# Weights first in SBUF and the other tiles 64 bytes behind multiples of 2048: a change of addresses alone in a convolution and squared-ReLU MLP kernel

## The chip, the cores and the metric

One core of one Trainium2 chip. The metric is the device time of one execution in microseconds (us); lower is better. The engines are named as in the profile: PE is TensorE's stream of matmuls, PEld its loads of stationary operands (weights), DVE is VectorE, ACT ScalarE, POOL GpSimd, SP SyncE. SBUF is the on-chip memory from which the engines read: 128 partitions side by side, and in each partition a row of bytes. An address below is the byte at which a tile begins in each partition.

## The reference, cut to what matters

```python
def _attn_ref(x, weight):            # x (8, 4096, 192), weight (8, 7)
    w = exp(weight - max(weight, -1)); w = w / (sum(w, -1) + 1e-09)
    x_pad = concatenate([zeros((B, 6, D)), x], axis=1)
    # out[b, s, h*24+g] = sum over k of w[h, k] * x_pad[b, s + k, h*24+g]

def _moe_ref(x, w_in, w_out, s, b):  # 32768 tokens, 192 -> 2048 -> 192
    h = x @ w_in
    r = np.maximum(h, 0.0)
    g = s * (r * r) + b
    return (g @ w_out).astype(np.float32)
```

A causal convolution with seven taps over the sequence is followed by two matrix products with a squared ReLU between them. The inputs are float32.

## The kernel before, in words

**Precision.** The kernel computes with float32 words marked fp32r and splits each operand into a high part and a low part, so that one product is three matmuls (high by low, low by high, high by high). The token tiles `sA`, `wA`, `tB`, `wB` hold both parts of the convolved tokens (`wA` and `wB` with the two partition halves swapped, filled by DMA at L171 and L172). `qh` and `ql` hold the high and low parts of the squares.

**Tiling.** Tokens go in blocks of 512 columns (`BLK`), two blocks to a super-block `n`. The 2048 hidden features go in eight pairs `p` of 2 x 128. One step is a triple `(n, j, p)`. A step has two groups of matmuls. `first` (L531) makes `h` of 256 features: nine products for each of two halves of 64 rows, so 18 matmuls. `second` (L614) multiplies the squares of an earlier step (two steps behind, `LAG = 2`) by the output weights: ten products for each half, so 20 matmuls. Almost all matmuls thus have 64 rows and come in couples: one of the couple uses partitions 0 to 63, the other 64 to 127, both stream 512 columns (2048 bytes of each partition), and they run side by side. Each has a weight load of its own, 128 columns (512 bytes of each partition). A step is 19 couples; a block of eight steps is 152 couples. The first super-block is different: it is done while weights are still being prepared, and its `second_whole` (L576 to L583) uses matmuls of the full 128 rows.

**Around the matmuls.** ACT takes `h` from PSUM with a ReLU (L545) and squares it (L552), DVE makes `qh` (L554) and `ql` (L559) and convolves the next block (L161, L163), POOL adds up the output halves (L638 to L647), SP issues the DMAs. The order on PE, DVE and ACT is the order in which the program was written; `queue` holds the squares that wait for `second`. In the first super-block the convolution of one part is done on PE with plain float32 operands (L257, `conv_tensor`).

**Where the tiles lie.** Tile pools are laid out in SBUF in the order in which they are opened, one behind the other, each tile rounded up to 32 bytes. The constants end 864 bytes behind a multiple of 2048, and the unused tile `gap` (L81, 296 words, 1184 bytes) fills the rest up to address 18432, which is 9 x 2048. From there on the pools follow: `qs` (ten tiles of 4096 bytes for `qh` and `ql`), `xs` (tokens), `act` (`q`), `outs`, `wide_w` (the weights `W`, 40960 bytes, at 139264, and `WB`, 8192 bytes, at 180224), `raw`, `wordp`, `xin`. All tiles up to `WB` have sizes that are multiples of 2048, so all begin at multiples of 2048. A 128-column slice of `W` or `WB`, as one weight load reads it, begins at a multiple of 512: `W` has rows of 640 words (2560 bytes) per pair and part, in slices of 128 words, and `WB` has rows of 128 words (512 bytes). So the slices fall on all four offsets 0, 512, 1024 and 1536 from a multiple of 2048, while every stream of 512 columns begins at an offset of 0.

Of the kernel before, what the change touches and what calls it, by code (L numbers as in the profile page):

```python
# [9 lines left out]
F32 = mybir.dt.float32  # L10
# [7 lines left out]
P = 128  # L18
# [9 lines left out]
WARM = (BLK, BLK // 2, BLK // 2)  # L28

GAP = 296  # L30


TOP_MIN = struct.unpack("<f", struct.pack("<I", (1023 - 127) << 20))[0]
# [4 lines left out]
def conv_attention_then_squared_relu_mlp(  # L38
# [40 lines left out]
    bb = const.tile([P, 1], F32, name="bb")  # L79
    bias = const.tile([P, 3], F32, name="bias")  # L80
    const.tile([P, GAP], F32, name="gap")  # L81
    qs = ctx.enter_context(tc.tile_pool(name="qs", bufs=LAG + 3))
    xs = ctx.enter_context(tc.tile_pool(name="xs", bufs=2))
    act = ctx.enter_context(tc.tile_pool(name="act", bufs=3))
    outs = ctx.enter_context(tc.tile_pool(name="outs", bufs=3))
    wide_w = ctx.enter_context(tc.tile_pool(name="wide_w", bufs=1))
    raw = ctx.enter_context(tc.tile_pool(name="raw", bufs=2))
    wordp = ctx.enter_context(tc.tile_pool(name="wordp", bufs=3))
    xin = ctx.enter_context(tc.tile_pool(name="xin", bufs=2))
# [759 lines left out]
```

## Time and profile before

| | |
|---|---|
| median of 3 runs | 2234.84 us (2234.82 to 2234.86) |
| the profiled execution's own time | 2234.66 us |
| its span, first to last instruction | 2232.9 us |
| PE busy | 2226.4 us, 19330 matmuls |
| PEld busy | 1829.1 us, 19330 loads |
| DVE busy | 1753.5 us |
| ACT busy | 1286.4 us |
| POOL busy | 317.8 us |
| granted TensorE clock | 1.000 of full |

A row of a group gives the line, engine, operation, output and inputs, their shapes and count, then the group's busy time in us and the mean duration of one in ns, then the idle time of the engine before them. Two matmuls that run side by side are both counted with their full duration there. The end of a matmul is modelled in these profiles, so its duration says little; the distance from one start to the next says how fast PE goes. A row of the timeline or of the chain gives the start in us, the length in us and what ran, with the count where several alike are merged. The span begins at 0.

### The profile page before, as it was taken

How to read it: one execution, taken by the hardware profiler on the slowest of the kernel's cores; microseconds unless marked ns; L12 is line 12 of the kernel's file. 1: busy time of each engine (PE TensorE's matmuls, PEld its weight loads, DVE VectorE, ACT ScalarE, POOL GpSimd, SP SyncE). 2: the span in 40 equal slices, each digit the busy share in tenths (PEclk: the TensorE clock that was granted, in tenths of full speed). 3: DMA queues.
4: the chain of work that ended last, by engine and by line, in shares of the span. 5: the costliest groups of instructions: out<-in, count | busy, mean ns of one | idle time of the engine just before them, and what ended most of it. 6: DMA issues, size and time to landing. Idle time of an engine off the chain costs nothing.

```text
span 2232.9 us, 45081 instructions
## 1 busy us (share of the span) xinstructions
PE 2226.4 (100%) x19330; PEld 1829.1 (82%) x19330; DVE 1753.5 (79%) x1995; ACT 1286.4 (58%) x1410; POOL 317.8 (14%) x205
## 2 busy tenths in 40 slices
PE   9999999999999999999999999999999999999999
PEld 6788888888888888888888888888888888888887
DVE  8898778777787787777877878778777787787764
ACT  8755555655555555555555555555655555556554
POOL 0022101111011011110110111111101111011110
PEclk9999999999999999999999999999999999999999
DMA  5113112121121111211111111112121121111110
GB/s 180 34 43 87 40 46 62 48 58 44 44 58 53 53 44 45 56 53 53 43 51 50 53 53 53 48 43 62 51 55 44 44 58 53 53 44 42 46 39 17
DMA packets 46168, 117.51 MB, mean 53 GB/s; under 512 B 7760, under 2 KB 8016, under 8 KB 45968
## 3 DMA queue, kind: packets, MB, share of 16 engines
q1 hardware_dynamic: 45824, 114.50, 18.6%
q8 instruction: 151, 2.47, 0.5%
q14 instruction: 49, 0.40, 0.1%
q10 hardware_dynamic: 144, 0.13, 0.0%
HBM read 31.64 MB, written 25.17 MB: 25 GB/s over the span
## 4 chain that ended last, share of the span: by engine, by line
PE 98%; DVE 1%; ACT 1%; DMA 0%; issue 0%; SPq 0%; DVEq 0%
PE acc L614 50%; PE h L531 46%; DVE accA L163 0%; PE acc L576 0%; ACT q L552 0%; DVE ql L559 0%; PE acc L577 0%; PE acc L583 0%; PE acc L582 0%; PE acc L581 0%; ACT qh L554 0%; ACT q L545 0%; DMA xA<-in_xA 0%; DVE t L315 0%; ACT oC L589 0%
## 5 line engine op out<-in xcount | busy, mean ns | idle before, releaser
L545 ACT ACTIVATE q<-h 128x1024 f32<-128x1024 f32 x512 | 525.5, 1026 | 902.8 <-PE h L531 900.4
L559 DVE TENSOR_TENSOR ql<-q,qh 128x1024 fp32r<-128x1024 f32 x512 | 656.7, 1283 | 56.3 <-ACT qh L554 2.6
L554 DVE CAST qh<-q 128x1024 fp32r<-128x1024 f32 x497 | 370.1, 745 | 395.7 <-ACT q L552 393.3
L614 PE MATMUL acc<-qh,W 64*128 64x512 f32 x3960 | 609.9, 386 | 0.0
L552 ACT ACTIVATE q<-q 128x1024 f32<-128x1024 f32 x512 | 543.6, 1062 | 15.9
L614 PEld LDWEIGHTS acc<-qh,W 64*128 64x128 f32 x3960 | 370.9, 184 | 77.9
L531 PE MATMUL h<-sA,W 64*128 64x512 f32 x3072 | 432.4, 387 | 0.0
L531 PE MATMUL h<-wA,W 64*128 64x512 f32 x3072 | 431.6, 386 | 0.0
L531 PE MATMUL h<-tB,W 64*128 64x512 f32 x1536 | 429.9, 386 | 0.0
L531 PE MATMUL h<-wB,W 64*128 64x512 f32 x1536 | 429.9, 386 | 0.0
L614 PE MATMUL acc<-ql,WB 64*128 64x512 f32 x1980 | 385.7, 386 | 0.4 <-DVE ql L559 0.4
L614 PE MATMUL acc<-qh,WB 64*128 64x512 f32 x1980 | 385.6, 386 | 0.0
L614 PE MATMUL acc<-ql,W 64*128 64x512 f32 x1980 | 385.5, 386 | 0.0
L638 POOL TENSOR_TENSOR oB<-oB,oB 128x512 f32<-128x512 f32 x61 | 115.2, 1889 | 1672.7 <-ACT oB L637 1672.7
L163 DVE SCALAR_TENSOR_TENSOR accA<-xA,tap,accA 128x512 f32<-128x512 f32 x378 | 341.5, 903 | 6.8
L531 PEld LDWEIGHTS h<-sA,W 64*128 64x128 f32 x3072 | 287.3, 184 | 62.9 <-issue 1.1
L531 PEld LDWEIGHTS h<-wA,W 64*128 64x128 f32 x3072 | 287.8, 184 | 60.4
L531 PEld LDWEIGHTS h<-tB,W 64*128 64x128 f32 x1536 | 282.6, 184 | 40.5 <-issue 0.2
L531 PEld LDWEIGHTS h<-wB,W 64*128 64x128 f32 x1536 | 282.5, 184 | 20.1
L614 PEld LDWEIGHTS acc<-ql,WB 64*128 64x128 f32 x1980 | 185.5, 184 | 40.1 <-DVE ql L559 1.3
L614 PEld LDWEIGHTS acc<-ql,W 64*128 64x128 f32 x1980 | 185.5, 184 | 39.0
L614 PEld LDWEIGHTS acc<-qh,WB 64*128 64x128 f32 x1980 | 185.5, 184 | 38.8
(115 smaller groups left out, 1035.4 us busy)
## 6 DMA issues: line engine op xcount, KB each, us to landing
wA<-sA SPq DMA_DIRECT2D x126, 256.0 KB, 3.6
outT<-oA SPq DMA_DIRECT2D x63, 256.0 KB, 2.0
wB<-tB SPq DMA_DIRECT2D x60, 256.0 KB, 3.4
xA<-in_xA SPq DMA_DIRECT2D x24, 515.0 KB, 3.6
xB<-in_xB SPq DMA_DIRECT2D x32, 259.0 KB, 2.6
oC<-oB SPq DMA_DIRECT2D x61, 128.0 KB, 2.2
outT<-oC SPq DMA_DIRECT2D x60, 128.0 KB, 2.3
words<-in_w SPq DMA_DIRECT2D x7, 768.0 KB, 6.2
```

What stands on the lines that cost most here:

```text
L163: nc.vector.scalar_tensor_tensor(acc, src, w[:, k : k + 1], acc, op0=ALU.mult, op1=ALU.add)
L531: nc.tensor.matmul(h[:, i, :], w_in(w, p, chunk[0], rows), chunk[part], start=start, stop=stop)
L545: nc.scalar.activation(q, h, AF.Relu)
L552: nc.scalar.activation(q, q, AF.Square)
L554: cast(qh, q)
L559: nc.vector.tensor_tensor(ql, q, qh.bitcast(F32), op=ALU.subtract)
L614: nc.tensor.matmul(accs[to + 2 * i], w(f, r), q[r, f % 2, :], start=start and f == 0, stop=stop and f == ends[i],)
L638: nc.gpsimd.tensor_tensor(o[1], o[1], o[3], op=ALU.add)
```

## The change

The pool of the weights is opened right behind `gap`, so `W` and `WB` come first. Behind them comes a new unused tile of 16 words (64 bytes), and then the other pools in their old order.

```diff
 GAP = 296
+SHIFT = 16
...
     const.tile([P, GAP], F32, name="gap")
+    wide_w = ctx.enter_context(tc.tile_pool(name="wide_w", bufs=1))
+
+    shift = ctx.enter_context(tc.tile_pool(name="shift", bufs=1))
+    shift.tile([P, SHIFT], F32, name="shift")
     qs = ctx.enter_context(tc.tile_pool(name="qs", bufs=LAG + 3))
     xs = ctx.enter_context(tc.tile_pool(name="xs", bufs=2))
     act = ctx.enter_context(tc.tile_pool(name="act", bufs=3))
     outs = ctx.enter_context(tc.tile_pool(name="outs", bufs=3))
-    wide_w = ctx.enter_context(tc.tile_pool(name="wide_w", bufs=1))
     raw = ctx.enter_context(tc.tile_pool(name="raw", bufs=2))
```

Worked out from the sizes: `W` begins at 18432 (9 x 2048) and `WB` at 59392 (29 x 2048), so weight slices still begin at multiples of 512. `qs` begins at 67648, 64 bytes behind 33 x 2048, and `qh`, `ql`, the token tiles, `q` and the outputs all begin 64 bytes behind a multiple of 2048. `raw`, `wordp` and `xin` move up by 64 bytes. No instruction is added, removed or put in another place.

## The prediction

> **What bounds the kernel now.** I read the page's busy times and clock row first, then the chain that ended last, then one steady window, then the chain in order of time inside it.
>
> ```profile
> span 2232.9 us, 45081 instructions
> PE 2226.4 (100%) x19330; PEld 1829.1 (82%) x19330; DVE 1753.5 (79%) x1995; ACT 1286.4 (58%) x1410; POOL 317.8 (14%) x205
> ...
> PEclk9999999999999999999999999999999999999999
> ...
> PE 98%; DVE 1%; ACT 1%; DMA 0%; issue 0%; SPq 0%; DVEq 0%
> PE acc L614 50%; PE h L531 46%; DVE accA L163 0%; PE acc L576 0%; ACT q L552 0%; DVE ql L559 0%; PE acc L577 0%; PE acc L583 0%; PE acc L582 0%; PE acc L581 0%; ACT qh L554 0%; ACT q L545 0%; DMA xA<-in_xA 0%; DVE t L315 0%; ACT oC L589 0%
> ```
>
> PE is busy all the time at the full granted clock, and 96% of the chain are the matmuls of L531 and L614. Who waits for whom confirms it:
>
> ```profile
> ACT q L545 <- PE h L531: 900.4, 372, 4.5
> ...
> PEld acc L614 <- DVE ql L559: 1.3, 2, 0.8
> ```
>
> ACT waits 900.4 us for PE's `h`; in the other direction the weight loads of L614 waited for `ql` twice, 1.3 us in all. So the time is the number of matmuls times the distance from one start to the next. That distance comes from a window and from two starts of the same row of the chain, one block apart:
>
> ```profile
> 104.00:2223.00 2119.00, 2119.00 (x18704) 1751.29 (x18704) 1657.91 (x1849) 1197.10 (x1290) 316.77 (x196) 1.00 0.18 50
> ...
> 165.01 4.08 PE h L531 x36
> 169.09 4.53 PE acc L614 x40
> ...
> 199.47 4.08 PE h L531 x36
> ```
>
> The window's columns are stretch, length, then busy us and count for PE, PEld, DVE, ACT and POOL, the clock, and the DMA share and GB/s. Its 18704 matmuls are all in couples but for eight tiny ones: 9348 couples in 2119.00 us, 226.7 ns each. From 165.01 to 199.47 are 34.46 us for the 152 couples of one block: 226.7 ns again. And the two groups agree: 4.08 us for 18 couples of `first`, 4.53 us for 20 of `second`, 226.7 and 226.5 ns. PE never pauses, so nothing but this 226.7 ns can move the time by much.
>
> **What is in the 226.7 ns.** A matmul here streams 512 columns of fp32r. In the head the same 512 columns go through PE as plain float32:
>
> ```profile
> 12.96 4.46 PE L257 MATMUL acc<-xA,q 128*128 128x512 f32 x10
> ...
> L257 PE MATMUL acc<-xA,q 128*128 128x512 f32 x14 | 6.3, 592 | 0.0
> ```
>
> The ten take 4.46 us from the first start to the modelled end of the last, which is given as 0.592 us long; that leaves 3.87 us for nine distances, 430 ns each. If such a matmul is two passes over the columns (the trace does not say so; it is the nearest reading of a duration just under twice the other), one pass costs 215 ns, and an fp32r couple costs 11.7 ns more than a bare pass. At 215 ns for 2048 bytes of a partition, 11.7 ns are the time of 111 bytes of stream, and 64 bytes are 6.7 ns.
>
> Beside each stream the load of the next weights is running:
>
> ```profile
> L614 PE MATMUL acc<-qh,W 64*128 64x512 f32 x3960 | 609.9, 386 | 0.0
> ...
> L614 PEld LDWEIGHTS acc<-qh,W 64*128 64x128 f32 x3960 | 370.9, 184 | 77.9
> L531 PE MATMUL h<-sA,W 64*128 64x512 f32 x3072 | 432.4, 387 | 0.0
> ...
> L531 PEld LDWEIGHTS h<-sA,W 64*128 64x128 f32 x3072 | 287.3, 184 | 62.9 <-issue 1.1
> L614 PEld LDWEIGHTS acc<-ql,WB 64*128 64x128 f32 x1980 | 185.5, 184 | 40.1 <-DVE ql L559 1.3
> ```
>
> A load is 184 ns long, shorter than the 226.7 ns between couples, so loads do not set the distance by their own length. They may set the extra 11.7 ns by reading SBUF at the same time as the stream: 512 bytes of weights and 2048 bytes of tokens or squares, all from addresses that are multiples of 512 (the layout above). That the extra belongs to the relation of load and stream in time is what these starts show:
>
> ```profile
> 36.42 0.40 PE L577 MATMUL acc<-ql,WB 128*128 128x512 f32 x1
> 36.66 0.40 PE L576 MATMUL acc<-qh,WB 128*128 128x512 f32 x1
> 36.89 0.40 PE L577 MATMUL acc<-ql,WB 128*128 128x512 f32 x1
> 37.13 0.39 PE L581 MATMUL acc<-qh,W 128*128 128x512 f32 x1
> 37.35 0.39 PE L582 MATMUL acc<-qh,W 128*128 128x512 f32 x1
> 37.58 0.40 PE L583 MATMUL acc<-ql,W 128*128 128x512 f32 x1
> 37.82 0.39 PE L581 MATMUL acc<-qh,W 128*128 128x512 f32 x1
> ...
> 38.51 0.39 PE L576 MATMUL acc<-qh,WB 128*128 128x512 f32 x1
> ```
>
> This is just behind a pause of PE. The first nine distances, 36.42 to 38.51, are 2.09 us, 232 ns each, and they scatter between 220 and 240 ns although form, weights and kinds of operand are those of the steady run. So the extra is no constant of the instruction: it goes up and down until the stream and the loads fall into a fixed step, and then stays at 226.7 ns.
>
> **The change part by part.** No instruction, wait or DMA is added, removed or moved in any queue; the two unused tiles are never read. Only addresses differ, so each part is a question whether an address is worth time.
>
> *Weights against streams.* Before, both begin at multiples of 512; after, the stream begins 64 bytes further. How many nanoseconds the couple gains or loses the trace of before can't show directly, as no stream in it stands 64 bytes off. Bounds: a gain of at most 11.7 ns, down to the 215 ns pass; a loss of 5.5 ns, up to the 232 ns of the starts that have not fallen into step. I take a gain of 6.7 ns, to 220.0 ns. The reasoning: if load and stream disturb each other where they touch the same piece of memory at once, then beginning both at the same offset is the worst arrangement, because they collide at the start, before the stream has run ahead; 11.7 ns are some two units of 64 bytes, and a stream that begins one unit ahead misses the first of the two. That is an estimate, worked out from the 430 ns and the 226.7 ns. The number of streams: 3960 + 6144 + 3072 + 5940 = 19116 matmuls of 64 rows (counts of L614 and L531 in the page), so 9558 couples, and 170 single ones of 128 rows in head and tail, 9728 in all. 9728 x 6.7 ns = 65 us. The ends are 9728 x 11.7 ns = 114 us gained and 9558 x 5.5 ns = 53 us lost.
>
> *The other engines' operands* (`q`, `qh`, `ql`, token tiles and outputs 64 bytes on, inputs too). I take nothing. Cover: at 220.0 ns the window of 2119 us would shrink to 2057 us, against 1657.91 us of DVE and 1197.10 us of ACT in it. DVE would have to slow down by 24% before it were late. Without that cover, each per cent on DVE would cost 17 us.
>
> *DMAs.* The swaps `wA<-sA` and the loads now touch SBUF 64 bytes off. They have a block of 34.46 us to arrive in:
>
> ```profile
> wA<-sA SPq DMA_DIRECT2D x126, 256.0 KB, 3.6
> ...
> xA<-in_xA SPq DMA_DIRECT2D x24, 515.0 KB, 3.6
> ...
> 1.65 3.28 DMA xA<-in_xA
> ```
>
> Landing takes 3.6 us, a tenth of the block. Only in the head does a transfer lie on the chain, 3.28 us for the first `xA`; even 10% on that is 0.3 us, either way.
>
> The sum against the profiled execution's own 2234.66 us: 2234.66 - 65 = 2169.7 us. Its own time lies 0.2 us under the median of the runs, so the forecast for the median is 2170 us, 2.9% less.
>
> **The rivals.** *No change.* The weight slices of before stand at four offsets from a multiple of 2048 (0, 512, 1024, 1536), and the streams at 0, yet `first` and `second`, `W` and `WB` all run at 226.7 ns. If four distances make no difference, a fifth may make none; the extra would then be the price of reading weights at all, wherever they lie. Against it: all four are multiples of 512, and a pattern that repeats every 512 bytes or less would look the same from each of them. Time: 2234.8 us. The Trainium skill sides with this rival: its page "TensorE: Matmul & The Clock Gate", Part 2, step 1, has PE read weights and stream through two independent SBUF ports, so that loading the next weights takes no read bandwidth from the running matmul; by that rule the sum is 0 and the time 2234.8 us. The scatter of 220 to 240 ns above speaks against reading it strictly, but does not show that addresses matter.
>
> *Slower: the fixed step is lost.* The steady 226.7 ns is better than the 232 ns that PE makes before it falls into step. With weights and streams at unequal offsets the pattern need not close on itself after each couple, and PE would go on as in the rows from 36.42 to 38.51. Price: 5.5 ns x 9558 = 53 us, 2288 us. It decides as soon as the steady distance stays above 226.7 ns; the place is every block from about 104 us on. For it: the scatter exists, and its mean is above the steady value. Against it: every restart in the head ends in the steady distance within about ten matmuls.
>
> *The whole extra goes.* If load and stream collide only because they begin together, the couple falls to 215 ns: 2235 - 114 = 2121 us. It is the far end of the forecast's case.
>
> **How the numbers follow.** Faster, as forecast, 0.50; no change 0.30; slower 0.20. The forecast's own range goes from the whole extra gone, 2121 us, to a gain of just over 0.2% (4.5 us, about the least that a measurement of this kernel can tell from no change), 2230 us. With the case of no change, up to 2239 us, eight in ten are held: 2120 to 2240 us. What is left out is the slower case.
>
> **What would show it.** In the chain of the changed kernel, right: one block of 152 couples in 33.4 us instead of 34.46 us, the same for `first` and `second`; PE still without pauses, ACT's wait for PE's `h` some 60 us shorter, DVE's and ACT's busy times unchanged. Wrong: a block still of 34.46 us (addresses do not matter at this distance); a block of about 35.3 us with distances that scatter (the step is lost); or PE waiting for `ql` or for a DMA, which would mean that the new addresses slow the other engines down. A distance that differs between `first` and `second`, or between `W` and `WB`, would mean that it is no common unit of 64 bytes but the particular pair of tiles that matters.

## The result, and the profile after

The changed kernel takes 2255.34 us (median of 4 runs, 2255.27 to 2255.94), against 2234.83 us of the kernel before beside it (4 runs, 2234.53 to 2234.86). The ratio is 1.0093, with a 95% interval from 1.008 to 1.0105: slower by 20.5 us, where the prediction had 65 us less.

The page of the changed kernel, with the rows that answer to those of before (`first` is now at L535, `second` at L618; in section 5 a row ends with busy time, mean duration of one in ns, and idle time before):

```profile
span 2253.6 us, 45081 instructions
PE 2247.3 (100%) x19330; PEld 1832.4 (81%) x19330; DVE 1755.5 (78%) x1995; ACT 1286.3 (57%) x1410; POOL 317.7 (14%) x205
...
PEclk9999999999999999999999999999999999999999
...
PE 98%; DVE 1%; ACT 1%; DMA 0%; issue 0%; SPq 0%; DVEq 0%
...
L563 DVE TENSOR_TENSOR ql<-q,qh 128x1024 fp32r<-128x1024 f32 x512 | 656.6, 1282 | 56.3 <-ACT qh L558 2.7
...
L618 PE MATMUL acc<-qh,W 64*128 64x512 f32 x3960 | 614.0, 388 | 0.0
...
L618 PEld LDWEIGHTS acc<-qh,W 64*128 64x128 f32 x3960 | 371.6, 184 | 81.7
...
wA<-sA SPq DMA_DIRECT2D x126, 256.0 KB, 3.7
```

Everything but PE is as it was, or nearly. DVE and ACT are busy as long as before, the clock is full, the swap's DMA takes 3.7 in place of 3.6 us, and each load still takes 184 ns. PE is busy for 20.9 us more, with the same 19330 matmuls. It is still the one that others wait for (who waited for whom, us in all, times, longest):

```profile
ACT q L549 <- PE h L535: 910.6, 371, 4.5
...
PEld acc L618 <- DVE ql L563: 1.1, 2, 0.6
```

The same window and the same piece of the chain as before give the distance between couples:

```profile
104.00:2223.00 2119.00, 2119.00 (x18524) 1737.43 (x18522) 1649.57 (x1839) 1187.73 (x1281) 314.65 (x195) 1.00 0.19 50
```

```profile
165.41 4.12 PE h L535 x36
169.53 4.58 PE acc L618 x40
...
200.20 4.12 PE h L535 x36
```

In the window are 18524 matmuls, 9258 couples without the eight tiny ones: 2119.00 / 9258 = 228.9 ns. A block takes 200.20 - 165.41 = 34.79 us, and 34.79 / 152 = 228.9 ns. `first` and `second` both have it (4.12 us for 18 couples, 4.58 us for 20). Against 226.7 ns that is 2.2 ns for each of 9558 couples, 21 us: the whole difference.

The times of the single starts in the trace, in ns, show how the 228.9 ns come about. These are distances from one couple's start to the next, 18 in succession in the steady part of each kernel:

```
before  226 227 227 226 227 227 226 227 227 226 227 227 226 227 227 226 227 227
after   229 231 226 229 232 226 229 232 226 229 231 226 229 232 226 229 232 226
```

Before, every couple is alike: 226.67 ns, rounded to whole ns. After, the couples go round in a cycle of three, 226, 229 and 232 ns, whose sum is 686.67 ns.

### The profile page after: what moved, and what is told of

The parts are those of the page before. It is cut to its first block, busy times and chain, and to the rows that moved or that the text cites. A ratio compares the mean times of both kernels' runs of the same rounds, so it can differ in the third digit from the quotient of the medians.

```text
span 2253.6 us, 45081 instructions
## 1 busy us (share of the span) xinstructions
PE 2247.3 (100%) x19330; PEld 1832.4 (81%) x19330; DVE 1755.5 (78%) x1995; ACT 1286.3 (57%) x1410; POOL 317.7 (14%) x205
## 4 chain that ended last, share of the span: by engine, by line
PE 98%; DVE 1%; ACT 1%; DMA 0%; issue 0%; SPq 0%; DVEq 0%
PE acc L618 50%; PE h L535 46%; DVE accA L167 0%; PE acc L580 0%; ACT q L556 0%; DVE ql L563 0%; PE acc L581 0%; PE acc L587 0%; PE acc L585 0%; PE acc L586 0%; ACT qh L558 0%; ACT q L549 0%; DMA xA<-in_xA 0%; DVE t L319 0%; ACT oC L593 0%
## 5 line engine op out<-in xcount | busy, mean ns | idle before, releaser
L618 PE MATMUL acc<-qh,W 64*128 64x512 f32 x3960 | 614.0, 388 | 0.0
L618 PEld LDWEIGHTS acc<-qh,W 64*128 64x128 f32 x3960 | 371.6, 184 | 81.7
L535 PE MATMUL h<-sA,W 64*128 64x512 f32 x3072 | 435.6, 389 | 0.0
L535 PE MATMUL h<-wA,W 64*128 64x512 f32 x3072 | 434.8, 388 | 0.0
L535 PE MATMUL h<-tB,W 64*128 64x512 f32 x1536 | 433.2, 388 | 0.0
L535 PE MATMUL h<-wB,W 64*128 64x512 f32 x1536 | 433.2, 388 | 0.0
L618 PE MATMUL acc<-ql,WB 64*128 64x512 f32 x1980 | 387.6, 388 | 0.2 <-DVE ql L563 0.2
L618 PE MATMUL acc<-qh,WB 64*128 64x512 f32 x1980 | 387.5, 388 | 0.0
L618 PE MATMUL acc<-ql,W 64*128 64x512 f32 x1980 | 387.4, 388 | 0.0
L535 PEld LDWEIGHTS h<-sA,W 64*128 64x128 f32 x3072 | 287.9, 184 | 65.6 <-issue 1.1
L535 PEld LDWEIGHTS h<-wA,W 64*128 64x128 f32 x3072 | 288.4, 184 | 63.2
L535 PEld LDWEIGHTS h<-tB,W 64*128 64x128 f32 x1536 | 283.1, 184 | 42.2 <-issue 0.2
L535 PEld LDWEIGHTS h<-wB,W 64*128 64x128 f32 x1536 | 283.1, 184 | 21.2
L618 PEld LDWEIGHTS acc<-ql,WB 64*128 64x128 f32 x1980 | 185.8, 184 | 41.8 <-DVE ql L563 1.1
L618 PEld LDWEIGHTS acc<-ql,W 64*128 64x128 f32 x1980 | 185.8, 184 | 40.8
L618 PEld LDWEIGHTS acc<-qh,WB 64*128 64x128 f32 x1980 | 185.8, 184 | 40.7
```

What stands on the lines that cost most here:

```text
L535: nc.tensor.matmul(h[:, i, :], w_in(w, p, chunk[0], rows), chunk[part], start=start, stop=stop)
L618: nc.tensor.matmul(accs[to + 2 * i], w(f, r), q[r, f % 2, :], start=start and f == 0, stop=stop and f == ends[i],)
```

## The experiments

Every kernel ran once, with a profile, beside a run of the kernel before on the same chip; those runs lie between 2234.36 and 2234.89 us. Below, offset is the distance in bytes from the start of a weight slice to the start of a stream, less all whole multiples of 256 (why 256, the row of offsets shows; the run with 256 itself is listed as such). The window quoted for each kernel is the same, from 300 to 2100 us: the count in the first pair of brackets is matmuls, half of it couples, and 1800 us divided by the couples is the distance. Matmuls that the ends of the window cut are counted too, so this is up to 0.1 ns less than what the single starts give. The times of single starts give the cycle, the row of distances that repeats. For the kernel before, and the changed one:

```profile
300.00:2100.00 1800.00, 1800.00 (x15886) 1487.66 (x15884) 1413.67 (x1568) 1021.17 (x1102) 262.75 (x165) 1.00 0.19 50
```

```profile
300.00:2100.00 1800.00, 1800.00 (x15730) 1475.83 (x15730) 1403.77 (x1555) 1008.22 (x1088) 259.77 (x162) 1.00 0.19 50
```

7943 and 7865 couples: 226.6 and 228.9 ns.

### Order, or streams' address, or offset?

Three theories stood against each other. A: the offset between weights and streams. B: the streams' own addresses. C: the place of the weights, now in front.

`e1_order`: weights first, without the 64 bytes.

```diff
-    shift = ctx.enter_context(tc.tile_pool(name="shift", bufs=1))
-    shift.tile([P, SHIFT], F32, name="shift")
```

> Weights first, but no 64 bytes: weights, squares, tokens and outputs all at multiples of 2048. If the offset between weight slices and streams is what counts (theory A), the distance between couples is 226.7 ns again and the time 2235 us. If the streams' own address counts, whatever the weights' (theory B), the same 2235 us. If the new place of the weights in memory counts (theory C), it stays at 228.9 ns and 2255 us.

`e2_all64`: the kernel before with everything behind the constants, weights too, 64 bytes on.

```diff
-GAP = 296
+GAP = 312
```

> The old order with everything, weights too, 64 bytes behind multiples of 2048, so that the offset between weights and streams is again a multiple of 512. Theory A (offset between the two): 226.7 ns, 2235 us. Theory B (the streams' own address): 228.9 ns in steps of 226, 229 and 232 ns, 2255 us. Theory C (place of the weights): 2235 us.

They took 2234.58 and 2234.60 us. The windows of `e1_order` and `e2_all64`:

```profile
300.00:2100.00 1800.00, 1800.00 (x15886) 1491.26 (x15884) 1414.78 (x1568) 1020.88 (x1102) 262.26 (x165) 1.00 0.19 50
```

```profile
300.00:2100.00 1800.00, 1800.00 (x15886) 1487.66 (x15884) 1414.77 (x1568) 1021.40 (x1102) 262.64 (x165) 1.00 0.19 50
```

Both have the 15886 matmuls of before. C falls with the first: weights in front cost nothing. B falls with the second: there every stream stands 64 bytes behind a multiple of 2048, as in the changed kernel, and nothing is lost, because the weights stand there too. Only A is left.

`e10_all32` put the same question for 32 bytes:

```diff
-GAP = 296
+GAP = 304
```

> The old order with everything 32 bytes behind multiples of 2048, weights too. If only the offset between weights and streams counts: 226.7 ns, 2234.5 us. If a stream or a slice also wants to begin at a multiple of 64 of its own: above 226.7 ns, up to the 233.3 ns and 2298 us that 32 bytes between them cost.

It took 2234.43 us, with a distance of 226.67 ns. So moving weights and streams together costs nothing, by 32 bytes as by 64.

### The row of offsets

Eight kernels change the offset and beyond it only addresses: seven are the changed kernel with another `SHIFT` (8, 24, 32, 40, 48, 56 or 64 words of 4 bytes), and one, `e12_w16`, leaves the order of before and moves the weights. In `e12_w16` both weight tiles also grow by 256 bytes, so the slices of `W` begin 16 bytes behind a multiple of 512, as its expectation says, but those of `WB` 272 bytes behind one; the offset is 240 for both.

```diff
-SHIFT = 16
+SHIFT = 8
```

```diff
-    W = wide_w.tile([P, NPAIR, 2, CB], F32R, name="W")
-    WB = wide_w.tile([P, NPAIR, 2, 2 * DB], F32R, name="WB")
+    W = wide_w.tile([P, NPAIR * 2 * CB + 64], F32R, name="W")[:, 4:][:, 0 : NPAIR * 2 * CB]
+    W = W.rearrange("p (n a c) -> p n a c", n=NPAIR, a=2)
+    WB = wide_w.tile([P, NPAIR * 4 * DB + 64], F32R, name="WB")[:, 4:][:, 0 : NPAIR * 4 * DB]
+    WB = WB.rearrange("p (n a c) -> p n a c", n=NPAIR, a=2)
```

32 bytes: 

> The change with 32 bytes in place of 64. Theory A: another offset, another step; somewhere between 215 and 236 ns and not 226.7 ns, with the best guess 232 ns (2287 us), since a piece of 64 bytes is now cut in two. Theory B: 228.9 ns or more, 2255 us or more. Theory C: 228.9 ns, 2255 us.

256 bytes: 

> The change with 256 bytes in place of 64. Theory A: if the pattern of load against stream repeats within 256 bytes, 226.7 ns and 2235 us; if it repeats only at 512 or more, another value, 220 to 232 ns. Theory B: 226.7 ns and 2235 us if the streams need a multiple of 128 or 256 only. Theory C: 228.9 ns, 2255 us.

128 bytes: 

> The change with 128 bytes. The offset between weights and streams counts, and 256 is as good as 0; if the pattern repeats every 128 bytes: 226.7 ns, 2234.5 us. If it repeats every 256: a value of its own, not 226.7 ns; 128 is then furthest from 0, best guess below 226.7 ns, 220 ns and 2170 us, if collisions are fewest there.

192 bytes: 

> The change with 192 bytes. If the pattern repeats every 128 bytes: the same as 64, 228.9 ns in the cycle 226, 229, 232, 2255 us. If it repeats every 256, 192 is 64 on the other side: another value than 228.9 ns is possible, between 215 and 233 ns.

96 bytes: 

> The change with 96 bytes. 32 bytes gave 233.3 ns (2298 us) and 64 gave 228.9 ns (2255 us). If odd multiples of 32 are bad because a stream no longer begins at a multiple of 64 against the weights: 233 ns and 2298 us. If the pattern is a curve over the offset with its low at 0 and 128 or 256: between 226.7 and 233 ns, other than 233.3.

Weights 16 bytes on: 

> The old order and place, but every weight slice begins 16 bytes behind a multiple of 512, so the streams stand 16 bytes before them (240 of 256). If the offset acts in pieces of 32 bytes or more: 226.7 ns, 2234.5 us. If it acts in pieces of 16 bytes or fewer: another steady cycle, 229 to 233 ns, 2255 to 2298 us.

160 bytes: 

> The change with 160 bytes. If 0 is the best of all offsets because a steady step closes there: 228 to 234 ns, 2250 to 2300 us. If another offset has a lower steady step: under 226.7 ns and under 2234.5 us.

224 bytes: 

> The change with 224 bytes. The same two cases as for 160 bytes; if the row of offsets is the same on both sides of 0, 233.3 ns and 2298 us as with 32.

| offset, bytes | run | time, us | distance, ns | steady cycle, ns |
|---|---|---|---|---|
| 0 | before | 2234.8 | 226.67 | 226.67, one couple |
| 32 | `e3_shift32` | 2298.07 | 233.33 | four couples, 933.33 |
| 64 | the change | 2255.34 | 228.89 | three couples, 686.67 |
| 96 | `e7_shift96` | 2297.84 | 233.33 | three couples, 700.00 |
| 128 | `e5_shift128` | 2288.93 | 232.38 | seven couples, 1626.67 |
| 160 | `e15_shift160` | 2306.91 | 234.29 | seven couples, 1640.00 |
| 192 | `e6_shift192` | 2297.95 | 233.33 | two couples, 466.67 |
| 224 | `e16_shift224` | 2297.92 | 233.33 | two couples, 466.67 |
| 240 | `e12_w16` | 2296.17 | 233.33 | six couples, 1400.00 |
| 256 | `e4_shift256` | 2234.26 | 226.67 | 226.67, one couple |

The windows of 32, 160 and 256 bytes stand for the others:

```profile
300.00:2100.00 1800.00, 1800.00 (x15432) 1443.18 (x15432) 1374.15 (x1521) 990.65 (x1068) 253.86 (x159) 1.00 0.18 49
```

```profile
300.00:2100.00 1800.00, 1800.00 (x15370) 1445.89 (x15368) 1367.23 (x1514) 989.06 (x1064) 253.60 (x159) 1.00 0.19 49
```

```profile
300.00:2100.00 1800.00, 1800.00 (x15886) 1487.64 (x15884) 1414.04 (x1568) 1021.58 (x1102) 263.56 (x165) 1.00 0.19 50
```

With 7716, 7685 and 7943 couples in the same 1800 us the distances are 233.3, 234.2 and 226.6 ns. At 256 bytes the distance of 0 is back. `e12_w16` agrees with a pattern of 256 bytes: its couples with `W` and those with `WB` differ by 256 bytes and run in one cycle. No other two offsets 256 bytes apart were compared. Of the nine offsets from 0 to 240, 0 is by far the best, and the change's 64 the second best. Even 16 bytes cost 61 us. The guesses that a far offset would beat 0 (down to 220 ns at 128 bytes) were all wrong, and of the versions that compute the same numbers none is clearly faster than the kernel before.

### One of the two streams off

`e9_squares64` keeps tokens and outputs at multiples of 2048 and moves only what lies from the squares on: the 64 bytes and the pool `qs` now come behind `outs`.

```diff
-    shift = ctx.enter_context(tc.tile_pool(name="shift", bufs=1))
-    shift.tile([P, SHIFT], F32, name="shift")
-    qs = ctx.enter_context(tc.tile_pool(name="qs", bufs=LAG + 3))
...
     outs = ctx.enter_context(tc.tile_pool(name="outs", bufs=3))
+    shift = ctx.enter_context(tc.tile_pool(name="shift", bufs=1))
+    shift.tile([P, SHIFT], F32, name="shift")
+    qs = ctx.enter_context(tc.tile_pool(name="qs", bufs=LAG + 3))
```

> Weights, tokens and outputs at multiples of 2048 and only the squares (and what lies behind them) 64 bytes further, so that only the streams of second are off. If each couple's own offset counts: first keeps 226.7 ns (18 couples in 4.08 us) and second has about 228.9 ns (20 couples in 4.58 us), a block of some 34.6 us, 2246 us. If the step runs through both groups and a break in one upsets the other: both above 226.7 ns, 2250 us or more. If what counts is the tokens' place or the outputs': 2234.5 us.

It took 2263.88 us, more than the change with all streams off, which is the second case of the expectation. In its chain both groups are slower than before (`first` is at L534, `second` at L617):

```profile
388.55 2.06 PE h L534 x18
390.61 2.31 PE acc L617 x20
392.92 2.06 PE h L534 x18
```

One step takes 392.92 - 388.55 = 4.37 us, 230.0 ns for each of its 19 couples; the nine couples of `first` have 229 ns and the ten of `second` 231. The starts show why (distances in ns, each line one group):

```
first   231 235 229 232 231 227 226 227 227
second  236 235 232 232 226 229 231 226 229 232
```

Each group runs into the cycle of its own offset, `first` into 226.67 and `second` into 226, 229, 232, but needs four or five couples of mostly 231 to 237 ns to get there, and then the other group takes over. So the offset acts couple by couple, and a change of offset costs a run-in each time.

### Loads with less to read

`e8_onecol` (from the kernel before) and `e18_onecol64` (from the changed one) let each load read its first column 128 times. The products are other numbers.

```diff
     def w_in(part, p, chunk, rows):
-        return W[rows, p, part, chunk * P : (chunk + 1) * P]
+        c = W[rows, p, part, chunk * P : chunk * P + 1]
+        return c.to_broadcast([c.shape[0], P])
```

(and `w_outA` and `w_outB` in the same way.)

> The kernel before, but each weight load reads its first column 128 times in place of 128 columns: the loads are as many and as long, but touch 4 bytes of each partition in place of 512. The products are other numbers. If the 11 ns over a bare pass come from loads and streams touching the same pieces of memory (theory A's mechanism): the distance changes from 226.7 ns, down to 215 ns (2121 us) if almost all collisions go. If they are the price of loading at all, or lie in the stream: 226.7 ns and 2234.5 us.

> The changed kernel with loads that read their first column 128 times (the products are other numbers). If the offset between load and stream acts even when the load stays at one address: another distance than the 231.7 ns of the same loads at offset 0. If it acts only through a load that runs along beside the stream: 231.7 ns, 2281 us.

`e11_half` lets most loads read 64 columns in place of 128, and so leaves half of those products out:

```diff
-                    h[:, i, :], w_in(w, p, chunk[0], rows), chunk[part], start=start, stop=stop
+                    h[0 : P if start or stop else HB, i, :],
+                    w_in(w, p, chunk[0], rows)[:, 0 : P if start or stop else HB],
+                    chunk[part], start=start, stop=stop
```

(and `second` in the same way.)

> The kernel before, but all products of the couples except the first and the last of each sum use 64 columns of the weights in place of 128, so the loads read 256 bytes of each partition in half the time; half of those products is left out. The change between 64 and 128 columns may cost PE pauses, so the distance is read inside runs of equal matmuls. If the extra over a bare pass comes from loads beside the streams: about half of the 11.7 ns goes, 220 to 221 ns. If it belongs to the stream itself: 226.7 ns.

The windows of `e8_onecol`, `e18_onecol64` and `e11_half`:

```profile
300.00:2100.00 1800.00, 1800.00 (x15548) 1509.38 (x15546) 1382.28 (x1533) 994.91 (x1073) 252.62 (x159) 1.00 0.18 49
```

```profile
300.00:2100.00 1800.00, 1800.00 (x15544) 1465.24 (x15542) 1381.48 (x1532) 995.38 (x1073) 254.96 (x159) 1.00 0.18 49
```

```profile
300.00:2100.00 1800.00, 1800.00 (x15670) 1108.14 (x15668) 1396.31 (x1548) 1004.54 (x1084) 258.65 (x162) 1.00 0.19 50
```

One-column loads give 231.5 ns at offset 0 (7774 couples, 2280.79 us) and 231.6 ns at offset 64 (7772 couples, 2281.82 us). Half loads, which take 131 ns each in place of 184 and bring the busy time on PEld down from 1487.66 to 1108.14 us, give 229.7 ns (7835 couples, 2263.28 us), and 229.8 ns between two matmuls that both have half loads. So what a load reads changes the distance, and the offset, at 0 against 64, no longer changes its mean when the load stays at one address. It still changes the pattern: at offset 64 the two matmuls of a couple begin 3 ns apart, in a cycle of four couples, while at offset 0 they come apart after about 160 us, begin some 45 ns apart (the median from 300 to 2100 us), and each goes round on its own. Less reading by the loads does not make PE faster, as collisions counted in bytes would have it. That a couple would become slower than 226.7 ns was in no case of the expectations for `e8_onecol` and `e11_half`.

### Streams with less to read

`e13_onestream` takes the other side: each stream of the couples reads its first column 512 times. `e14_both` does it with one-column loads. `e17_twice` reads 256 columns, each twice in succession. All three compute other numbers.

```diff
-                    h[:, i, :], w_in(w, p, chunk[0], rows), chunk[part], start=start, stop=stop
+                    h[:, i, :], w_in(w, p, chunk[0], rows),
+                    chunk[part][:, 0:1].to_broadcast([HB, BLK]), start=start, stop=stop
```

```diff
+                    chunk[part][:, 0 : BLK // 2].unsqueeze(2).to_broadcast([HB, BLK // 2, 2]),
```

(and `second` in the same way.)

> The kernel before, but the couples' streams read their first column 512 times in place of 512 columns (the products are other numbers); the loads are as before. If the extra over a bare pass comes from the stream reading its 2048 bytes beside the load: 213 to 217 ns, a time of about 2121 us. If it comes from the load or from the matmul itself: 226 ns or more.

> Loads and streams both read one column again and again. If the extra comes from reading the memory, on either side: 213 to 217 ns, about 2121 us. If it is in the matmul itself or in reading at all, whatever the address: 226 ns or more; if one address read by both is the worst collision: well above 233 ns.

> The kernel before, but each stream reads 256 columns, every one twice in succession, in place of 512 (the products are other numbers): the same length at half the rate of new bytes, beside full loads. If the rate of new bytes is what makes a stream late: 215 to 217 ns, about 2125 to 2137 us, as with one column. If any reading of changing addresses does it: 220 ns or more.

The windows, in the same order:

```profile
300.00:2100.00 1800.00, 1800.00 (x16660) 1576.81 (x16658) 1464.24 (x1630) 1066.33 (x1146) 264.63 (x169) 1.00 0.19 52
```

```profile
300.00:2100.00 1800.00, 1800.00 (x16656) 1577.28 (x16654) 1463.75 (x1630) 1065.68 (x1146) 264.17 (x169) 1.00 0.19 52
```

```profile
300.00:2100.00 1800.00, 1800.00 (x16682) 1578.99 (x16680) 1467.09 (x1631) 1071.41 (x1149) 271.62 (x170) 1.00 0.19 52
```

8330, 8328 and 8341 couples: 216.1, 216.1 and 215.8 ns, and 2136.79, 2137.17 and 2135.81 us. The 10.6 ns above 216.1 appear only where a stream of fp32r reads a new column at every step. At half the rate of new columns, beside full loads, they are gone.

## Why the prediction was wrong, point by point

**What bounds the kernel: right.** PE without pauses, in a fixed distance between couples, made the time before and makes it after. The other engines and the DMAs were rightly taken at nothing: their busy times did not move, and `e2_all64`, which moves all their operands by 64 bytes too, cost nothing.

**What is in the 226.7 ns: half right.** That a couple can pass in about 215 ns is borne out by `e17_twice` (215.8 ns); that plain float32 goes in two passes remains a reading. The distances behind a pause were read from rows rounded to 10 ns, and from matmuls of 128 rows, not of the form of the steady run. The single starts bear the reading out all the same: from 36.42 us on they are 235, 233, 236, 224, 231, 236, 228, 233 and 230 ns apart, so 224 to 236 and not 220 to 240, and the couples of `first` that begin behind pauses, at 31.76 and 40.87 us, go through the same distances, to within 1 ns, before they settle. But the extra was put down to collisions whose number grows with what the loads read. Half loads (229.7 ns) and loads of one column (231.5 ns) speak against that.

**The step that failed** is this one: "beginning both at the same offset is the worst arrangement", and with it the "two units of 64 bytes", of which a shift by one would save the first. The gain of 6.7 ns for each couple that was worked out from it was a loss of 2.2 ns, and the row of offsets shows the opposite of the premise: the same offset is the best of nine. The size of the extra suggested the unit of 64 bytes, and nothing in the trace of before showed such a unit. The starts behind the pauses, with 232 ns on average, were the one sight that the trace gave of matmuls out of step, and eight of the nine distances lie above 226.7 ns. That was the warning.

**The slower rival had the mechanism, at too high a price.** It said that at unequal offsets the pattern need not close on itself after each couple. It does not: it closes after three, with 226, 229 and 232 ns. The term that was mis-sized is the distance: 232 ns was taken, the mean of matmuls that run in, for 53 us; the steady cycle has 228.9 ns, 2.2 ns more than before, which times 9558 is 21 us. At other offsets the rival's price was near: 232.4 ns at 128 bytes, 233.3 ns at 32. The sign named for it was a block of about 35.3 us with distances that scatter; the profile shows 34.79 us, and distances that go round in a cycle and do not scatter.

**The rival of no change** reasoned from the four offsets of the weight slices (0, 512, 1024, 1536) that a fifth distance may make no difference. The objection noted there, that a pattern of 512 bytes or less looks the same from each of them, was the point: 256 bytes more bring the 226.67 ns back. The Trainium skill (the page "TensorE: Matmul & The Clock Gate", Part 2, step 1) says that weights and stream come through two independent ports, so that loading the next weights takes no read bandwidth from the running matmul. The sum of 0 that was drawn from this did not come: with the order and the streams' addresses unchanged, moving the weights by 16 bytes modulo 256 (`e12_w16`) took a couple from 226.7 to 233.3 ns. Whether it is read bandwidth that the load takes is not shown; loads that read half as much did not make PE faster.

**The rival that the whole extra goes** was reached at no offset. Only streams with fewer new columns to read came to 216 ns.

**What stays open.** Why the cycle at offset 0 closes after one couple, and which structure of the memory has the 256 bytes, is not settled. Whether a stream with no load beside it would run in 216 ns was not tried: each matmul here brings its own load. The streams that repeat a column also have another access pattern, and no run separates that from the lower rate of new columns. That 226.67 ns is a low point because a steady step closes there is a reading of the cycles, not something that a run took apart.

## What to carry to other kernels

Where PE never pauses, look at the distances between single matmul starts and not only at their mean: here a constant distance was a step that load and stream kept together, and a change of addresses broke it. In a kernel like this one, let weight slices and streams of fp32r begin at the same remainder modulo 256 bytes, and all streams that follow each other too, since in `e9_squares64` each change of offset cost a run-in of four or five couples. A steady value that the trace shows in thousands of instances may already be the good end of its range; the out-of-step rows beside it are a hint on which side of it the other arrangements lie.

## What the runs showed of the hardware that was not expected

Every steady cycle of the row of offsets is a whole number of 6.667 ns: 34 of them for one couple at offset 0 (226.67 ns), 103 for three at 64, 140 for four at 32, 105 for three at 96, 244 for seven at 128, 246 for seven at 160, 70 for two at 192 and 224, 210 for six at 240. In the kernel before, all 14 stretches of steady distance in the first 115 us (at least six in succession), most of them behind pauses of PE, begin within 0.7 ns of the same point of such a beat. So the streams of fp32r seem to keep time with a beat of 6.667 ns that goes on through PE's pauses. The streams of `e17_twice`, with half as many new columns, do not: their steady 215.83 ns are 32.4 beats. At the 215.8 ns that 512 columns, 2048 bytes of stream, take there, one beat is 63 bytes. What the beat is the runs do not tell.
